# Squared-ReLU attention and a gated MLP on one core: 24 more score tiles of the first batch are written out and read back transposed, GpSimd copying their halves

## The chip, the cores and the metric

The kernel runs on one core of a Trainium2 chip. The time is the device time of one execution in microseconds (us). The engines are PE (TensorE), DVE (VectorE), ACT (ScalarE), POOL (GpSimd) and SP, whose instruction queue issues every transfer of this kernel.

## The reference

```python
scores = (1 / S) * z @ z.T            # per batch, S = 3008, z is S x 64
attn = maximum(scores, 0) ** 2
x = u * (attn @ v)                    # u and v are S x 256
xn = x / sqrt(mean(x * x) + 1e-6) * rms_g
y = (silu(xn @ w_gate) * (xn @ w_val)) @ w_out    # d_ff = 1536
```

There are four batches, and z, u and v are float32. The three weight matrices arrive as float64 and are used as two float32r parts each (a high and a low part), and so is every other operand of a product.

Scores are symmetric, so the tile of rows k and columns q is the transpose of the tile of rows q and columns k. The kernel makes use of that.

## The kernel before, in words

The tokens of a batch are cut into 6 chunks of 512 columns (the last has 448), and a chunk's keys into 24 tiles of 128 rows (the last has 64). A **step** is one key tile of one chunk; there are 4 x 6 x 24 = 576 steps, numbered i, and a program written out by hand goes through them in order. What an engine or SP's queue gets is in program order, and each works through its own queue in order.

In iteration i the program emits, in this order: the scores of step i + 3 (`emit_s`, L274 on: two matmuls at L284 and L285, the ReLU on ACT at L287 into a tile r, of which there are three); the preparation parts due at i (`stages`); the splitting of step i + 2 (`emit_l`, L296 on); the loads due at i (`loads`); a part of the MLP (`emit_g`, `emit_v`, `emit_y`), two iterations to one hidden tile of 128, from iteration 56 on; and the six matmuls of step i that multiply by v (`emit_av`, L342, L343, L347). In the first 80 steps most tiles are squared on ACT in `emit_l` (L302 writes H, L303 squares r in place); for the others DVE multiplies (L289) and ACT casts (L305). DVE subtracts the high part (L308, L313 for the last key tile).

**Kept tiles.** `keeps(b, c, kc)` names the groups of four key tiles (kc) that chunk c writes out for later: for these, behind the subtraction in `emit_l`, ACT copies the square r as two planes of 16-bit halves into a tile `halves` (L321; two buffers, which the result tiles y share), and SP's queue writes `halves` to device memory (L323, 256 KB). Chunk kc later needs the transpose of this block, in its four steps of key group c (`is_turned`, L259), and computes no score there: `load_turned` (L264 on) reads two steps at once with a transposing transfer into a tile T, six steps ahead, and L284 to L289 fall away. Before the change, `keeps` holds from step 72 on: 12 tiles of the first batch and 60 of each other batch (192 copies, 192 turned steps).

**Weights.** Each of the 18 pieces of weights is loaded by SP's queue (L114, 512 KB, into one of three buffers that T shares) in the loads of an iteration a - 3 and decoded and split in iterations a - 1 to a + 2. The first part is a square on ACT (`magnitude`, L122), then come seven instructions on DVE (L126 to L143) and a cast on ACT (L137). With a = 21, 25, 29, 33, 37, 41, 45, 49, 53, and then every second iteration to 71, the loads stand in iterations 18, 22, 26, 30, 34, 38, 42, 46, 50, 52, ..., 68. The moving operand z of the next chunk (`prep_mov`, L168) is loaded in iterations 18, 42 and 66, ahead of the weights of that iteration, and split on DVE (L173, L175) two iterations later. The u of a chunk (L357) is loaded at its 19th step.

A piece of the order in which `emit_l` and the loads are emitted, on which SP's queue depends:

```python
run(stages, i)
if i + LA <= nsteps and not ends:
    emit_l(i + LA - 1)
run(loads, i)
```

Of the kernel before, what the change touches and what calls it, by code (L numbers as in the profile page):

```python
# [12 lines left out]
U16 = mybir.dt.uint16  # L13
# [17 lines left out]
def kernel(  # L31
# [13 lines left out]
    nc = tc.nc  # L45
# [6 lines left out]
    NK = -(-S // P)  # L52
    NC = -(-S // CH)
# [4 lines left out]
    SKEW = 16  # L58
# [23 lines left out]
    def f32(ap):  # L82
        return ap.bitcast(F32)
# [170 lines left out]
    def keeps(b, c, kc):  # L254


        return (b * NC + c) * NK + 4 * kc >= NK + 3 * SKEW

    def is_turned(i):  # L259
        ci, kt = steps[i]  # L260
        b, c = chunks[ci][:2]
        return kt // 4 < c and keeps(b, kt // 4, c)
# [29 lines left out]
    def is_square(i):  # L292

        return i < 2 * NK + 2 * SKEW and (i % 6 != 5 if i < NK else i % 8 != 7)

    def emit_l(i):  # L296
        ci, kt = steps[i]
        b, c, t0, n = chunks[ci]
        a = att[i]
        hi = moving.tile([P, CH], F32R, tag="H", name="H", bufs=LA)  # L300
        if is_square(i):
            nc.scalar.activation(hi[:, :n], a[:, :n], AF.Square)  # L302
            nc.scalar.activation(a[:, :n], a[:, :n], AF.Square)  # L303
        else:
            nc.scalar.copy(hi[:, :n], a[:, :n])  # L305
        if kt < NK - 1:
            lo = moving.tile([P, CH], F32R, tag="L", name="L", bufs=LA)
            nc.vector.tensor_tensor(lo[:, :n], a[:, :n], f32(hi[:, :n]), op=ALU.subtract)  # L308
        else:

            lo = None
            h = slice(TAIL, P)
            nc.vector.tensor_tensor(hi[h, :n], a[h, :n], f32(hi[h, :n]), op=ALU.subtract)  # L313
        att[i] = (hi, lo)
        kc = kt // 4
        if kc > c and keeps(b, c, kc):
            if kt % 4 == 0:
                kept[b, kc, c] = dram.tile([2 * CH, CH], U16, tag=f"kept{kc}{c}", name=f"kept{kc}{c}")
            m = P if kt < NK - 1 else TAIL
            halves = work.tile([P, 2, CH], U16, tag="out", name="halves", bufs=2)  # L320
            nc.scalar.copy(halves[:m], a[:m].bitcast(U16).rearrange("p (q h) -> p h q", h=2))  # L321
            r0 = 2 * (kt % 4) * P
            nc.sync.dma_start(  # L323
                out=kept[b, kc, c][r0:r0 + 2 * m, :].rearrange("(p h) q -> p h q", h=2), in_=halves[:m]
            )
# [230 lines left out]
    def moe_at(fs):  # L556

        ci, f = divmod(fs, NF)
        return (ci, f) if 0 <= ci < len(chunks) else None
# [9 lines left out]
    with tc.manual_schedule():  # L569
# [12 lines left out]
        for i in range(LA):  # L582
            emit_s(i)
            if i:
                emit_l(i - 1)
            if early:
                run(stages, early.pop(0))
        for i in range(nsteps + 2 * (SKEW + NF + 1)):
# [9 lines left out]
# [3 lines that stand above are left out]
            m = moe_at(fs)  # L601
# [5 lines left out]
            m = moe_at(fs - 1)  # L607
# [8 lines left out]
            if ends:  # L616
                emit_gate(ci)
                if i + LA <= nsteps:
                    emit_l(i + LA - 1)
                for k, part in enumerate(norm_jobs(ci)):  # L620
                    stages[i + 1 + k].append(part)
# [33 lines left out]
```

## Time and profile before

| | us |
|---|---|
| median of 3 runs | 2138.23 (2137.46 to 2138.39) |
| the profiled execution | 2138.34 |
| its span, first to last instruction | 2136.6 |
| busy: PE, DVE, ACT, POOL | 2114.5, 1308.3, 1165.3, 0.2 |

The profiled execution lies within the three runs, and 1.7 us of it lie outside the span. Busy time is the share of the span in which an engine had an instruction running. Matmuls overlap each other in the profile: one is shown with 390 ns, but they start about 225 ns apart. An idle time is put down to the last thing that the instruction behind it waited for.

### The profile page before, as it was taken

The numbers are of one execution on the slowest core, as the hardware profiler recorded it, in microseconds if no ns is written. First come the engines' busy times: TensorE is split into PE (matmuls) and PEld (weight loads), VectorE is DVE, ScalarE is ACT, GpSimd is POOL, SyncE is SP. The second block draws the span as 40 slices with busy tenths as digits, with TensorE's granted clock in tenths as the row PEclk, the third lists the DMA queues.
The fourth block names the chain that finished last, engine by engine and source line by source line (L and its number), as shares of the span: only waits on it lengthen the run. The fifth ranks groups of instructions, "written<-read, shape, count | busy, mean of one in ns | idle before, by whom it ended". The sixth has DMA issues, their size and how long they took to land.

```text
span 2136.6 us, 25456 instructions
## 1 busy us (share of the span) xinstructions
PE 2114.5 (99%) x9408; PEld 1762.6 (82%) x9408; DVE 1308.3 (61%) x2361; ACT 1165.3 (55%) x1979; POOL 0.2 (0%) x4
## 2 busy tenths in 40 slices
PE   8899999999999999999999999999999999999999
PEld 7677888888888888888888888888888888888888
DVE  7988655775565555576655555557656565555543
ACT  8876555446574554545756545444666564544332
POOL 0000000000000000000000000000000000000000
PEclk9999999999999999999999999999999999999999
DMA  4211021322241415261313143244131332415100
GB/s 134 75 59 45 25 57 39 89 65 79 62 118 42 116 44 107 54 150 51 108 44 106 44 96 87 65 106 114 65 87 56 85 93 56 101 51 100 27 11 19
DMA packets 255660, 156.78 MB, mean 73 GB/s; under 512 B 198256, under 2 KB 213744, under 8 KB 255536
## 3 DMA queue, kind: packets, MB, share of 16 engines
q1 hardware_dynamic: 255536, 155.16, 26.8%
q8 instruction: 73, 1.20, 0.2%
q14 instruction: 51, 0.42, 0.1%
HBM read 46.60 MB, written 60.42 MB: 50 GB/s over the span
## 4 chain that ended last, share of the span: by engine, by line
PE 93%; DVE 4%; ACT 2%; issue 1%; DMA 0%; DVEq 0%
PE ps L460 12%; PE ps L461 12%; PE ps L463 12%; PE po L343 11%; PE po L342 11%; PE po L347 11%; PE py L496 6%; PE py L498 6%; PE py L497 6%; PE ps L285 4%; PE ps L284 4%; DVE L L308 1%; DVE wraw L128 0%; ACT H L302 0%; DVE wraw L141 0%
## 5 line engine op out<-in xcount | busy, mean ns | idle before, releaser
L482 ACT CAST hH<-s 128x512 fp32r<-128x512 f32 (+1 forms) x288 | 176.2, 612 | 526.0 <-DVE s L481 525.8
L342 PE MATMUL po<-H,vh 128*128 128x512 f32 (+1 forms) x1152 | 445.3, 387 | 0.0
L343 PE MATMUL po<-H,vl 128*128 128x512 f32 (+1 forms) x1152 | 445.2, 386 | 0.0
L289 DVE TENSOR_TENSOR r<-ps,r 128x512 f32<-128x512 f32 (+1 forms) x315 | 215.0, 683 | 309.2 <-ACT r L287 309.0
L287 ACT ACTIVATE r<-ps 128x512 f32<-128x512 f32 (+1 forms) x384 | 227.0, 591 | 278.6 <-PE ps L285 275.1
L347 PE MATMUL po<-L,vh 128*128 128x512 f32 (+1 forms) x1104 | 338.4, 388 | 5.6 <-DVE L L308 5.5
L483 DVE TENSOR_TENSOR hL<-s,hH 128x512 fp32r<-128x512 f32 (+1 forms) x288 | 196.2, 681 | 195.3 <-ACT hH L482 195.3
L481 DVE TENSOR_TENSOR s<-ps,s 128x512 f32<-128x512 f32 (+1 forms) x288 | 194.3, 675 | 191.4 <-PE ps L463 191.0
L308 DVE TENSOR_TENSOR L<-r,H 128x512 fp32r<-128x512 f32 (+1 forms) x360 | 243.8, 677 | 31.9 <-ACT r L303 20.4
L342 PEld LDWEIGHTS po<-H,vh 128*128 128x128 f32 x1152 | 216.8, 188 | 42.0 <-DVE H L313 0.4
L343 PEld LDWEIGHTS po<-H,vl 128*128 128x128 f32 x1152 | 216.9, 188 | 41.5
L347 PEld LDWEIGHTS po<-L,vh 128*128 128x128 f32 x1104 | 206.1, 188 | 51.2 <-DVE L L308 13.4
L496 PE MATMUL py<-hH,woh 128*128 128x512 f32 (+1 forms) x576 | 223.7, 388 | 4.4 <-ACT hH L482 4.3
L460 PE MATMUL ps<-xh,wvh 128*128 128x512 f32 (+1 forms) x576 | 224.5, 390 | 0.0
L498 PE MATMUL py<-hL,woh 128*128 128x512 f32 (+1 forms) x576 | 223.4, 388 | 0.0
L461 PE MATMUL ps<-xh,wvl 128*128 128x512 f32 (+1 forms) x576 | 222.4, 386 | 0.0
L470 ACT ACTIVATE s<-ps 128x512 f32<-128x512 f32 (+1 forms) x288 | 169.8, 590 | 96.3 <-PE ps L463 82.7
L497 PE MATMUL py<-hH,wol 128*128 128x512 f32 (+1 forms) x576 | 222.3, 386 | 0.0
L461 PE MATMUL ps<-xh,wgl 128*128 128x512 f32 (+1 forms) x576 | 222.2, 386 | 0.0
L460 PE MATMUL ps<-xh,wgh 128*128 128x512 f32 (+1 forms) x576 | 222.2, 386 | 0.0
L321 ACT COPY halves<-r 128x1024 uint16<-128x1024 uint16 x192 | 201.0, 1047 | 3.6 <-DMA out_T<-y 3.6
L305 ACT CAST H<-r 128x512 fp32r<-128x512 f32 (+1 forms) x315 | 191.3, 607 | 0.2 <-PE po L343 0.2
(81 smaller groups left out, 2655.5 us busy)
## 6 DMA issues: line engine op xcount, KB each, us to landing
kept<-halves SPq DMA_DIRECT2D x175, 256.0 KB, 2.0
raw<-in_v SPq DMA_DIRECT2D x44, 256.0 KB, 2.8
ux<-in_uT SPq DMA_DIRECT2D x40, 256.0 KB, 3.0
out_T<-y SPq DMA_DIRECT2D x40, 256.0 KB, 2.0
raw<-in_zT SPq DMA_DIRECT2D x39, 256.0 KB, 3.0
wraw<-in_w_gate SPq DMA_DIRECT2D x6, 512.0 KB, 5.4
wraw<-in_w_val SPq DMA_DIRECT2D x6, 512.0 KB, 3.5
wraw<-in_w_out SPq DMA_DIRECT2D x6, 512.0 KB, 3.2
```

Of the source, the lines that this page charges most:

```text
L287: nc.scalar.activation(a[:, :n], ps[:, :n], AF.Relu)
L289: nc.vector.tensor_tensor(a[:, :n], ps[:, :n], a[:, :n], op=ALU.mult)
L308: nc.vector.tensor_tensor(lo[:, :n], a[:, :n], f32(hi[:, :n]), op=ALU.subtract)
L342: nc.tensor.matmul(po[d][:, :n], wh[:, j, ds], hi[:, :n], start=(kt == 0), stop=False)
L343: nc.tensor.matmul(po[d][:, :n], wl[:, j, ds], hi[:, :n], start=False, stop=(lo is None))
L347: nc.tensor.matmul(po[d][:, :n], wh[:, j, ds], lo[:, :n], start=False, stop=False)
L460: nc.tensor.matmul(ps[:, :n], hi[:, d, fs], xsplit[ci, d][0][:, :n], start=(d == 0), stop=False)
L461: nc.tensor.matmul(ps[:, :n], lo[:, d, fs], xsplit[ci, d][0][:, :n], start=False, stop=False)
L463: nc.tensor.matmul(ps[:, :n], hi[:, d, fs], xsplit[ci, d][1][:, :n], start=False, stop=(d == ND - 1))
L496: nc.tensor.matmul(py[d][:, :n], woh[:, f, ds], hi[:, :n], start=(f == 0), stop=False)
L497: nc.tensor.matmul(py[d][:, :n], wol[:, f, ds], hi[:, :n], start=False, stop=False)
L498: nc.tensor.matmul(py[d][:, :n], woh[:, f, ds], lo[:, :n], start=False, stop=(f == NF - 1))
```

## The change

It makes `keeps` true for the groups kc = 4 and 5 of the first batch in every chunk, where it was true from step 72 on, and leaves the other batches as they are. New are the key tiles 16 to 23 of the chunks 0, 1 and 2 (steps 16 to 23, 40 to 47 and 64 to 71). The halves of the steps before 72 are copied by GpSimd in place of ACT; those are the 24 new ones and no others.

```diff
     def keeps(b, c, kc):
 
 
-        return (b * NC + c) * NK + 4 * kc >= NK + 3 * SKEW
+        return b > 0 or kc >= 4
 
     def is_turned(i):
         ci, kt = steps[i]
@@ -318,7 +318,9 @@
                 kept[b, kc, c] = dram.tile([2 * CH, CH], U16, tag=f"kept{kc}{c}", name=f"kept{kc}{c}")
             m = P if kt < NK - 1 else TAIL
             halves = work.tile([P, 2, CH], U16, tag="out", name="halves", bufs=2)
-            nc.scalar.copy(halves[:m], a[:m].bitcast(U16).rearrange("p (q h) -> p h q", h=2))
+
+            copy = nc.gpsimd.tensor_copy if i < 3 * NK else nc.scalar.copy
+            copy(halves[:m], a[:m].bitcast(U16).rearrange("p (q h) -> p h q", h=2))
             r0 = 2 * (kt % 4) * P
             nc.sync.dma_start(
                 out=kept[b, kc, c][r0:r0 + 2 * m, :].rearrange("(p h) q -> p h q", h=2), in_=halves[:m]
```

## Rows read from the trace of the kernel before

**Rows 1.** The page, busy time of each engine over the span.
```profile
PE 2114.5 (99%) x9408; PEld 1762.6 (82%) x9408; DVE 1308.3 (61%) x2361; ACT 1165.3 (55%) x1979; POOL 0.2 (0%) x4
```

**Rows 2.** Windows over steps 16-23, 40-47, 64-71: stretch, length, busy by engine, clock, DMA.
```profile
37.50:51.00 13.50, 12.82 (x56) 10.06 (x55) 11.46 (x20) 12.12 (x22) 0.00 (x0) 1.00 0.54 194
90.64:105.00 14.36, 11.20 (x43) 7.84 (x43) 13.20 (x23) 12.37 (x24) 0.00 (x0) 0.94 0.49 167
160.50:187.00 26.50, 26.16 (x109) 19.45 (x107) 22.01 (x39) 18.05 (x33) 0.00 (x0) 1.00 0.27 90
```

**Rows 3.** The chain that ended last, 92 to 95 us: start, length, piece.
```profile
92.92 0.57 ACT woh L122
93.49 0.53 ACT H L302
94.04 0.64 ACT r L303
94.70 0.69 DVE L L308
```

**Rows 4.** Timeline of DVE, L364 at a chunk's end: batches 0 and 1, chunks 3-5.
```profile
291.48 1.28 DVE L364 TENSOR_TENSOR ux<-po,ux 128x512 f32<-128x512 f32 x2
381.84 1.28 DVE L364 TENSOR_TENSOR ux<-po,ux 128x512 f32<-128x512 f32 x2
468.26 1.15 DVE L364 TENSOR_TENSOR ux<-po,ux 128x448 f32<-128x448 f32 x2
819.63 1.28 DVE L364 TENSOR_TENSOR ux<-po,ux 128x512 f32<-128x512 f32 x2
904.64 1.28 DVE L364 TENSOR_TENSOR ux<-po,ux 128x512 f32<-128x512 f32 x2
987.25 1.15 DVE L364 TENSOR_TENSOR ux<-po,ux 128x448 f32<-128x448 f32 x2
```

**Rows 5.** Timeline of PE, two score matmuls of 512 columns in chunk 4.
```profile
339.41 0.39 PE L284 MATMUL ps<-mh,zst 128*128 128x512 f32 x1
339.63 0.39 PE L285 MATMUL ps<-ml,zst 128*128 128x512 f32 x1
```

**Rows 6.** Groups of instructions, first 500 us: operation, shapes, count, busy, mean ns, idle before.
```profile
L308 DVE TENSOR_TENSOR L<-r,H 128x512 fp32r<-128x512 f32 (+1 forms) x136 | 92.0, 677 | 21.8 <-ACT r L303 20.4 <-ACT H L305 0.9 <-PE ps L285 0.3
L321 ACT COPY halves<-r 128x1024 uint16<-128x1024 uint16 (+1 forms) x19 | 19.9, 1046 | 0.0
```

**Rows 7.** Timeline of SP's queue (start, length, issue), and L114's time to landing, first 200 us.
```profile
41.48 0.90 SPq L114 DMA_DIRECT2D wraw<-in_w_gate  x2
...
90.02 0.94 SPq L357 DMA_DIRECT2D ux<-in_uT  x2
91.01 0.42 SPq L168 DMA_DIRECT2D raw<-in_zT  x1
91.49 2.42 SPq L114 DMA_DIRECT2D wraw<-in_w_gate  x2
...
DMA to landing us min/median/max: 3.1/3.4/7.6
```

**Rows 8.** Timeline of ACT around the first weight squares (L122) in the kept stretches.
```profile
44.04 0.63 ACT L303 ACTIVATE r<-r 128x512 f32<-128x512 f32 x1
...
47.47 0.67 ACT L122 ACTIVATE wgh<-wraw 128x512 fp32r<-128x512 f32 x1 [0.34 <-DMA wraw<-in_w_gate]
...
90.01 0.63 ACT L303 ACTIVATE r<-r 128x512 f32<-128x512 f32 x1
...
92.81 0.68 ACT L122 ACTIVATE woh<-wraw 128x512 fp32r<-128x512 f32 x1
...
98.46 0.63 ACT L303 ACTIVATE r<-r 128x512 f32<-128x512 f32 x1
...
101.14 0.66 ACT L122 ACTIVATE wgh<-wraw 128x512 fp32r<-128x512 f32 x1
...
168.18 0.63 ACT L303 ACTIVATE r<-r 128x512 f32<-128x512 f32 x1
...
174.65 0.66 ACT L122 ACTIVATE wvh<-wraw 128x512 fp32r<-128x512 f32 x1
```

**Rows 9.** Windows, 103 to 106 us, columns as in rows 2.
```profile
103.00:106.00 3.00, 2.71 (x7) 1.99 (x7) 2.90 (x6) 1.10 (x2) 0.00 (x0) 0.56 0.32 131
```

## The prediction

> **What bounds the kernel now.** The page comes first: PE is busy for 99% of the span and GpSimd does nothing [rows 1]. A score less is therefore worth its time on PE wherever PE really is the limit. But the copies that pay for it lie in the first 190 us, so I read that stretch apart. In the windows over the three stretches of new copies DVE is busy 11.46 of 13.50, 13.20 of 14.36 and 22.01 of 26.50 us, and ACT nearly as much in the first two [rows 2]. The chain of waits in the second goes from a weight square on ACT (L122) through the squares of a step to L308 on DVE, without PE [rows 3]. So here ACT and DVE set the pace, in turn, and a wait put on either is paid at the end. The chunks 4 and 5, where scores go, are bound by PE: its matmuls follow each other at 0.22 us [rows 5].
>
> **The gain: 24 turned steps in chunks 4 and 5.** `is_turned` asks the same function as `emit_l`, so the count is sure: 48 matmuls go, 24 of 512 columns and 24 of 448. The profile holds the very case: batch 1 already turns all these steps. From the end of chunk 3 to the end of chunk 4 it takes 904.64 - 819.63 = 85.01 us in batch 1 and 381.84 - 291.48 = 90.36 us in batch 0; chunk 5 takes 82.61 and 86.42 us [rows 4]. The difference is 5.35 + 3.81 = **9.2 us**. The other way, 24 x 0.22 + 24 x 0.22 x 448/512, gives 9.9 (10.2 with 0.227 us, since the rows are rounded) [rows 5]. I take 9.2. The 24 ReLUs, 24 multiplications and 12 transposing loads that change there lie beside PE as they do in batch 1; the loads come six steps ahead, and their blocks were written some 150 us before.
>
> **How long is a GpSimd copy?** No row shows one. The same copy on ACT takes 1.046 us; DVE does 512 elements in 0.677, so 1024 would take 1.35 [rows 6]. I take 1.4, the plain one-element-at-a-time pace, nearest to a copy of 1024 small elements; the ends are 1.05 and 2.7 (half that pace). The Trainium skill, "GPSIMD Engine Reference", "Performance versus the Vector engine", measures 512 elements of a one-input loop at 769 ns; doubled, that is an estimate of 1.54 us, which would add 0.14 to each lateness below. ACT saves nothing here, since these copies were not on it.
>
> **The wait that the change adds: weight loads behind a kept write.** SP's queue gets the kept write of step i + 2 ahead of the loads of iteration i, and the write waits for the copy. Before, SP ran far ahead: the first weights were issued at 41.48 us, and a weight pair at 91.49, which is when the u load in front of it let go [rows 7]; one late item holds all behind it. Now the load of iteration 18 stands behind the write of step 20, that of 38 behind step 40 and that of 42 behind step 44. Each lands after: end of r + copy 1.4 + issue 0.4 (0.4 more where the z load stands between) + 3.4 to land [rows 7]. Against the start of L122, which waits in ACT's queue ahead of the next steps' squares [rows 8]:
> - iteration 18: r ends 44.67, landing 44.67 + 1.4 + 0.8 + 3.4 = 50.3; L122 stood at 47.47: 2.8 us late.
> - iteration 38: 90.64 + 1.4 + 0.4 + 3.4 = 95.8 against 92.81: 3.0 late, and this L122 is in the chain [rows 3].
> - iteration 42: 99.09 + 1.4 + 0.8 + 3.4 = 104.7 against 101.14: 3.6 late.
>
> Together 9.4 us. The z load of 18 and 42 lands 0.4 us ahead of the weights and is wanted by DVE in the same iteration: inside the same stall. Behind the late square wait H and r of the step, L308, the weight's own seven DVE instructions and PE, which all lack it, so I count **9.4 us** in full. With the lower copy and the shortest landing (3.1) it is 3 x 0.65 less, 7.4; with a copy of 2.7 it is 13.3, and one landing of 7.6 would make it 17.5. The loads of 22 and 46 have two more iterations behind the last kept write: nothing. In chunk 2 steps last longer: r ends at 168.81, landing 174.0, L122 at 174.65 [rows 8]; four such loads are just in time, 0; at 2.7 us a copy they cost some 0.6 each. The u and v loads of chunk 0 come one or two copies later and are needed steps later: nothing.
>
> **GpSimd beside DVE.** Copy and L308 are released by the same end of r and read the same tile. Whether they slow each other no row shows. Lower end 0: the copies on ACT leave L308 at its 677 ns [rows 6]. Upper end: the two never overlap. Then 24 x 1.4 = 33.6 us of copies must fit into DVE's idle time, 2.04 + 1.16 + 4.49 = 7.7 [rows 2], and into the 9.4 us of stalls, and 16.5 us are left over; at 2.7 us a copy, 44. I take **5**, nearer to zero, as the only row of a copy says, but not zero, because the two start together each time.
>
> **Smaller terms.** PE's granted clock was 0.56 in the window behind a pause of PE near 102 us [rows 9]: seven matmuls there took about 0.43 in place of 0.225 us, 1.4 us. The first two new pauses may each do this, beside ACT and DVE: 0 to 2.8, taken **1.4**. The r tile must be free for the ReLU three steps on, some 1.85 us after its end; a copy of 1.4 fits (0), one of 2.7 would hold up 16 steps by 0.85, 14 us. The 24 writes of 256 KB share the rings with loads: DMA is busy 54% at most [rows 2]; inside the landing times.
>
> **Sum.** -9.2 + 9.4 + 5 + 1.4 = +6.6. The profiled execution took 2138.34 us, 1.7 beyond its span of 2136.6 and 0.1 above the median of the runs, so **2145.0 us**. A measurement of this kernel tells 0.2%, 4.3 us, from no change; this is just beyond.
>
> **The rivals.**
> *The two engines exclude each other.* For it: common start, DVE 85 to 92% busy. Against it: nothing in the profile shows any such exclusion. Its price is the upper end above: -9.2 + 9.4 + 16.5 + 1.4 = +18, **2156 us**; with copies of 2 us some 14 more. It decides once DVE loses over half a copy each time. The Trainium skill, "SBUF — State Buffer", "Who interferes with whom", says just this: a VectorE instruction with two SBUF inputs, or in a two-port mode, and a GpSimd instruction that reads SBUF exclude each other for the whole of whichever starts first. L308 and the weight arithmetic have two such inputs. No run here shows it yet. By that rule I would say 2156, and I give it a good chance. 0.27.
> *They cancel.* No effect on DVE and no lost clock: -9.2 + 9.4 = 0, **2138 us**. For it: L308's constant duration. 0.17.
> *Faster: the idle time takes up the stalls.* ACT has 1.38 and 1.99 us idle in the first two stretches [rows 2], waiting for others; if a late L122 only takes the place of these waits, and copy and landing are at their short ends, 7.4 - 3.4 = 4.0 us remain of the stalls and with the gain at 10.2 the result is -6.2, **2132 us**. It decides when the three stalls and all else cost under 4.9. Against it: L122 lies in the chain itself [rows 3]. 0.21.
> That the change does something else than it says is ruled out by the common function. 0.
>
> **How the numbers follow.** The forecast's own case, stalls and a mild hindrance of DVE, runs from +4.3 to +12 (2142.6 to 2150) and gets 0.35. Slower: 0.35 + 0.27 = 0.62; within 0.2%: 0.17; faster: 0.21. The range must take in the faster rival and most of the excluding one with copies of up to 2 us: **2132 to 2170**; below lies a full gain without stalls, above it copies of 2.7 us, about a tenth each.
>
> **What would show it.** Right: 24 GpSimd copies near 1.4 us; SP's weight loads of iterations 18, 38 and 42 issued right behind kept writes; ACT idle for about 3 us in front of three L122, released by the DMA; the ends of chunks 4 and 5 9 us closer together; L308 beside a copy a little longer than 677 ns or started later. The end of chunk 2 would come some 16 us later than before. Wrong: L122 never waiting for a load; L308 lengthened by a whole copy (then the first rival); chunks 4 and 5 unchanged.

## The result, and the profile after

The changed kernel takes 2151.84 us (median; 2151.09 to 2152.18), the kernel before 2137.85 on the same chip: a ratio of 1.0064, 95% interval 1.0052 to 1.0076, or some **14 us slower**. The profiled execution has a span of 2149.9 us, 13.3 more than before.

The page's busy times [rows 1]: 48 matmuls are gone, GpSimd works for 32.5 us, and DVE is busy for longer although 24 of its multiplications fell away.

```profile
PE 2106.6 (98%) x9360; PEld 1752.5 (82%) x9360; DVE 1314.0 (61%) x2337; ACT 1153.5 (54%) x1955; POOL 32.7 (2%) x28
```

The timeline of DVE, the line at the end of each chunk (L366 now), chunks 0 to 5 of batch 0 [rows 4]:

```profile
63.78 1.28 DVE L366 TENSOR_TENSOR ux<-po,ux 128x512 f32<-128x512 f32 x2
128.81 1.28 DVE L366 TENSOR_TENSOR ux<-po,ux 128x512 f32<-128x512 f32 x2
223.71 1.28 DVE L366 TENSOR_TENSOR ux<-po,ux 128x512 f32<-128x512 f32 x2
314.00 1.28 DVE L366 TENSOR_TENSOR ux<-po,ux 128x512 f32<-128x512 f32 x2
399.02 1.28 DVE L366 TENSOR_TENSOR ux<-po,ux 128x512 f32<-128x512 f32 x2
481.63 1.15 DVE L366 TENSOR_TENSOR ux<-po,ux 128x448 f32<-128x448 f32 x2
```

From one end to the next, in us (chunk 0 from the span's start). The kernel before has its ends at 56.31, 111.71, 199.91 and then as in [rows 4]. The runs told of below have their lines here too, by the names they have there:

| kernel | 0 | 1 | 2 | 3 | 4 | 5 |
|---|---|---|---|---|---|---|
| before | 56.31 | 55.40 | 88.20 | 91.57 | 90.36 | 86.42 |
| changed | 63.78 | 65.03 | 94.90 | 90.29 | 85.02 | 82.61 |
| Loads early | 61.96 | 60.13 | 94.90 | 90.30 | 85.02 | 82.61 |
| Copies alone | 60.74 | 60.77 | 94.88 | 91.62 | 90.36 | 86.41 |
| Chunk 2 on ACT | 63.32 | 65.11 | 89.40 | 90.31 | 85.02 | 82.60 |
| VectorE copies | 63.36 | 65.81 | 94.56 | 90.34 | 85.02 | 82.61 |
| Both mends (early, GpSimd and ACT) | 62.08 | 59.86 | 88.59 | 90.28 | 85.01 | 82.61 |
| Only chunk 2 (on ACT) | 56.23 | 55.39 | 88.41 | 89.77 | 88.55 | 84.77 |
| VectorE in chunks 0 and 1 (early, ACT in chunk 2) | 62.95 | 59.50 | 89.15 | 90.32 | 85.02 | 82.62 |
| Half copies | 57.84 | 57.15 | 91.52 | 91.61 | 90.36 | 86.42 |
| Memsets | 57.53 | 54.63 | 90.13 | 91.59 | 90.36 | 86.42 |
| ACT throughout (early) | 63.24 | 61.29 | 88.74 | 90.28 | 85.02 | 82.60 |
| All mended | 60.59 | 59.25 | 88.24 | 88.49 | 85.02 | 82.61 |

The change loses 7.47 + 9.63 + 6.70 = 23.8 us in chunks 0 to 2 and wins 1.28 + 5.34 + 3.81 = 10.4 in chunks 3 to 5. The two leave 13.4 us, against 13.3 between the spans.

Two things are new in chunks 0 to 2. First, ACT waits for weights. The timelines of ACT (L122, the first weight square; in brackets the idle time before it) and of SP's queue (L325 is the kept write, L168 the z load, L114 the weight load) show the three places [rows 7, 8]:

```profile
53.99 0.69 ACT L122 ACTIVATE wgh<-wraw 128x512 fp32r<-128x512 f32 x1 [4.60 <-DMA wraw<-in_w_gate]
...
103.57 0.66 ACT L122 ACTIVATE woh<-wraw 128x512 fp32r<-128x512 f32 x1 [2.45 <-DMA wraw<-in_w_out]
...
119.03 0.67 ACT L122 ACTIVATE wgh<-wraw 128x512 fp32r<-128x512 f32 x1 [5.37 <-DMA wraw<-in_w_gate]
```

```profile
48.16 0.34 SPq L325 DMA_DIRECT2D kept<-halves  x1
48.62 0.37 SPq L168 DMA_DIRECT2D raw<-in_zT  x1
49.03 0.45 SPq L114 DMA_DIRECT2D wraw<-in_w_gate  x1
...
99.29 0.34 SPq L325 DMA_DIRECT2D kept<-halves  x1
99.74 0.38 SPq L114 DMA_DIRECT2D wraw<-in_w_out  x1
...
113.06 0.34 SPq L325 DMA_DIRECT2D kept<-halves  x1
113.44 0.43 SPq L168 DMA_DIRECT2D raw<-in_zT  x1
114.32 0.33 SPq L114 DMA_DIRECT2D wraw<-in_w_gate  x1
```

A kept write stands in front, in the first and the third with the z load between, as the prediction had it. The first weights were issued at 41.48 us before, at 49.03 now.

Second, DVE and GpSimd stand in each other's way. The timelines of DVE and of GpSimd over two copies in chunk 2, where no load is late:

```profile
177.69 0.68 DVE L308 TENSOR_TENSOR L<-r,H 128x512 fp32r<-128x512 f32 x1
178.29 1.53 DVE L141 TENSOR_TENSOR wraw<-wraw,wgh 128x512 f32<-128x512 f32 x1
179.74 0.41 DVE L126 TENSOR_SCALAR wt<-wraw 128x512 uint32<-128x512 uint32 x1
180.07 1.52 DVE L143 TENSOR_TENSOR wgl<-wraw 128x512 fp32r<-128x512 f32 x1
181.52 0.68 DVE L128 SCALAR_TENSOR_TENSOR wraw<-wraw,wt 128x512 uint32<-128x512 uint32 x1
```

```profile
177.70 1.57 POOL L323 COPY halves<-r 128x1024 uint16<-128x1024 uint16 x1 [54.03 <-ACT r L303]
179.86 1.19 POOL L323 COPY halves<-r 128x1024 uint16<-128x1024 uint16 x1 [0.58 <-ACT r L303]
```

L141 and L143 take 1.53 and 1.52 us in place of 0.69. The first copy is shown from 177.70 on, beside L308, behind which L141 starts at 178.29; the copy ends at 179.27, and L141 ends 0.55 later, at 179.82. So the shown durations hold a wait: copy behind L308, L141 behind the copy. The copies' durations in the first 230 us agree (count, minimum, median and maximum in ns):

```profile
L323 POOL COPY halves<-r x24: 1042/1452/1572, 37.5 to 209.0; 128x1024 uint16<-128x1024 uint16 x21, 64x1024 uint16<-64x1024 uint16 x3
```

The least, 1.04 us, is a copy with nothing in its way. Each copy here costs DVE 1.53 - 0.69 = 0.84 us, and eight of them 6.7, which is the whole loss of chunk 2 (6.70).

### The profile page after: what moved, and what is told of

The parts are those of the page before. It is cut to its first block, busy times and chain, and to the rows that moved or that the text cites. A ratio compares the mean times of both kernels' runs of the same rounds, so it can differ in the third digit from the quotient of the medians.

```text
span 2149.9 us, 25445 instructions
## 1 busy us (share of the span) xinstructions
PE 2106.6 (98%) x9360; PEld 1752.5 (82%) x9360; DVE 1314.0 (61%) x2337; ACT 1153.5 (54%) x1955; POOL 32.7 (2%) x28
## 4 chain that ended last, share of the span: by engine, by line
PE 91%; DVE 4%; ACT 2%; issue 1%; DMA 1%; POOL 0%; SPq 0%; DVEq 0%; ACTq 0%; POOLq 0%
PE ps L462 12%; PE ps L463 12%; PE ps L465 12%; PE po L345 11%; PE po L344 11%; PE po L349 10%; PE py L498 6%; PE py L500 6%; PE py L499 6%; PE ps L284 3%; PE ps L285 3%; DVE L L308 1%; ACT H L302 1%; DVE wraw L128 1%; ACT r L287 1%
## 5 line engine op out<-in xcount | busy, mean ns | idle before, releaser
L289 DVE TENSOR_TENSOR r<-ps,r 128x512 f32<-128x512 f32 (+1 forms) x291 | 199.3, 685 | 285.6 <-ACT r L287 285.2
L287 ACT ACTIVATE r<-ps 128x512 f32<-128x512 f32 x360 | 213.3, 593 | 254.9 <-PE ps L285 248.7
L308 DVE TENSOR_TENSOR L<-r,H 128x512 fp32r<-128x512 f32 x336 | 232.3, 692 | 34.4 <-ACT r L303 22.3
L498 PE MATMUL py<-hH,woh 128*128 128x512 f32 (+1 forms) x576 | 223.6, 388 | 12.1 <-ACT hH L484 12.1
L305 ACT CAST H<-r 128x512 fp32r<-128x512 f32 (+1 forms) x291 | 177.3, 609 | 0.2 <-PE po L345 0.2
```

The costliest lines, as they stand in the source:

```text
L287: nc.scalar.activation(a[:, :n], ps[:, :n], AF.Relu)
L498: nc.tensor.matmul(py[d][:, :n], woh[:, f, ds], hi[:, :n], start=(f == 0), stop=False)
```

## The experiments

**Loads early.** It takes the late weights away and leaves the copies.

```diff
-            plan(prep_w(*w), at - 1, 2)
+            plan(prep_w(*w), at - 1, 8 if at < NK + 2 * SKEW - 3 else 2)
```

> The changed kernel with the first eight weight loads issued six iterations earlier (8 instead of 2 iterations ahead of their first use), so that none of them stands behind the kept write of the step that it needs. Theory: two costs add up, the late loads (ACT waited 4.6, 2.5 and 5.4 us for them, 12.1 us more than before) and GpSimd's copies holding up VectorE (the rest of the 23.8 us lost in chunks 0 to 2, 11.7 us). Then those waits go and the time falls by 8 to 12 us, to 2140 to 2144 us, still slower than before (2137.9). Rival, exclusion alone: the stalls only hide the copies, which then hold up VectorE for as long; the time falls by under 4 us, 2148 us or more. Rival, loads alone: back to the full gain, about 2128 us.

2144.72 us, ratio to the kernel before 1.0032 (1.0020 to 1.0044): 7.1 less than the changed kernel. No L122 waits for a transfer any more. The 12.1 us of waits were worth 7.1 by the times and 6.7 by the chunks (chunk 0: 1.8, chunk 1: 4.9, chunk 2: nothing), just below the theory's 8. That part of the waits had covered time that DVE loses to the copies anyway is the likely reason; it was not measured by itself. What lies behind is still slower than before, so loads alone (2128) is out, and so is exclusion alone.

**Copies alone.** The other half by itself, added to the kernel before, with no gain and no new transfers.

```diff
+        if kc > c and kc >= 4 and not keeps(b, c, kc):
+            m = P if kt < NK - 1 else TAIL
+            halves = work.tile([P, 2, CH], U16, tag="out", name="halves", bufs=2)
+            nc.gpsimd.tensor_copy(halves[:m], a[:m].bitcast(U16).rearrange("p (q h) -> p h q", h=2))
```

> The kernel before plus the 24 GpSimd copies and nothing else: no kept writes of them and no turned steps, so no gain and no late load. Theory: VectorE is held up once per copy by about 0.84 us (1.53 in place of 0.69 us for one instruction beside each), 24 x 0.84 = 20 us less what VectorE's idle time takes up: plus 12 to 18 us, 2150 to 2156 us. Rival (the copies hinder VectorE little, the loads are all): plus 5 us or less, below 2143 us.

2154.95 us, ratio 1.0080 (1.0063 to 1.0097): **16.5 us** for copies that nobody reads. By chunk 4.4, 5.4 and 6.7. This and the 7.1 of the loads make up the 23.8 us lost, but for 0.2 (but for 0.6 by the chunks). DVE's groups in the first 210 us, two-input instructions beside copies (mean ns at the end; 687, 690 and 689 in the kernel before):

```profile
L308 DVE TENSOR_TENSOR L<-r,H 128x512 fp32r<-128x512 f32 x69 | 52.1, 760 | 14.8 <-ACT r L303 14.1 <-PE ps L285 0.5
L143 DVE TENSOR_TENSOR wol<-wraw 128x512 fp32r<-128x512 f32 x4 | 3.5, 868 | 0.1
L143 DVE TENSOR_TENSOR wgl<-wraw 128x512 fp32r<-128x512 f32 x6 | 5.8, 969 | 0.1
```

What part has TensorE's clock in it? The windows over chunk 2, first of "loads early", then of this run, bear on it (columns as in rows 2): the granted clock is 1.00 in one and 0.96 in the other, DVE is busy equally long, and the chunk takes the same time, so the lower clock shows no cost there. Busy DVE explains the length: 76.24 us in chunk 2 of the kernel before, 83.00 here.

```profile
122.09:216.99 94.90, 81.44 (x335) 60.62 (x333) 83.00 (x142) 59.83 (x110) 10.98 (x8) 1.00 0.26 79
121.51:216.39 94.88, 84.11 (x335) 62.85 (x333) 83.00 (x142) 59.83 (x110) 10.89 (x8) 0.96 0.18 59
```

**Half copies.** The same with one of the two planes, half the elements: does the cost go by the copy's length or by the meeting?

```diff
-            nc.gpsimd.tensor_copy(halves[:m], a[:m].bitcast(U16).rearrange("p (q h) -> p h q", h=2))
+            nc.gpsimd.tensor_copy(halves[:m, 0, :], a[:m].bitcast(U16).rearrange("p (q h) -> p h q", h=2)[:, 0, :])
```

> The kernel before plus 24 GpSimd copies of one of the two planes, half the elements of a full copy (no kept writes, no turned steps, as in the run of copies alone, which lost 16.5 us). Theory (a VectorE instruction beside a copy waits for the copy's length): about half of a full copy's 1.04 us alone, so some 0.3 to 0.5 us per copy are lost on VectorE in place of 0.84, plus 6 to 10 us, 2144 to 2148 us. Rival (each meeting of the two costs a fixed time, whatever the length): plus 13 us or more, 2151 us or above.

2145.16 us, ratio 1.0035 (1.0021 to 1.0049), 6.8 us for 24 half copies. The least duration of a copy fell from 1.04 to 0.62 us, the lengthened L141 from 1.53 to 1.10. In chunk 2 3.3 us are lost in place of 6.7. The cost goes by the length.

**Memsets.** Does GpSimd have to read for it? A memset of the same tile in place of the copy, started by a tiny VectorE copy so that it begins just behind L308.

```diff
-            nc.gpsimd.tensor_copy(halves[:m], a[:m].bitcast(U16).rearrange("p (q h) -> p h q", h=2))
+            nc.vector.tensor_copy(halves[:m, 0, :2], a[:m, :1].bitcast(U16))
+            nc.gpsimd.memset(halves[:m], 0)
```

> The run of copies alone with each GpSimd copy replaced by a GpSimd memset of the same 128x1024 tile, which reads nothing; a VectorE copy of two elements of r into the tile goes before it, so that it starts at the same place (24 times some 0.17 us on VectorE). It tells whether the exclusion needs GpSimd to read. Theory (it is the read that VectorE's second input waits for): the instructions of VectorE with two tensor inputs (L141, L143, L128, L136) keep their 0.69 us beside a memset, and the time is 2 to 6 us above the kernel before, 2140 to 2145 us. Rival (any GpSimd instruction that uses the memory excludes VectorE's): they are lengthened as beside a copy, and 12 us or more are lost, 2150 us or above. The Trainium skill, "SBUF — State Buffer", "Who interferes with whom", says that an instruction with two inputs contends with a GpSimd instruction that reads, not with one that only writes, while a two-port one (the casts and tensor-scalar instructions of 0.42 us) contends with both.

2141.56 us, ratio 1.0016 (1.0006 to 1.0025): 3.4 us, with the 24 tiny copies (0.17 each) in it. By chunk 1.2, -0.8 and 1.9. DVE's groups as above:

```profile
L308 DVE TENSOR_TENSOR L<-r,H 128x512 fp32r<-128x512 f32 x73 | 50.1, 687 | 16.5 <-ACT r L303 16.4
L126 DVE TENSOR_SCALAR wt<-wraw 128x512 uint32<-128x512 uint32 x18 | 9.0, 501 | 0.0
L143 DVE TENSOR_TENSOR wol<-wraw 128x512 fp32r<-128x512 f32 x6 | 4.1, 690 | 0.1
```

And one place in the timelines, first GpSimd's memset, then DVE:

```profile
170.60 0.95 POOL L320 MEMSET halves<- 128x1024 uint16 x1 [3.90 <-DVE halves L319]
170.44 0.69 DVE L141 TENSOR_TENSOR wraw<-wraw,wgh 128x512 f32<-128x512 f32 x1
171.04 0.79 DVE L126 TENSOR_SCALAR wt<-wraw 128x512 uint32<-128x512 uint32 x1
```

L141, with two inputs, runs beside the memset in its usual 0.69 us; L126, an instruction of 0.42 us with one input, takes 0.79. So it is GpSimd's read that the two-input instructions wait for, and the quick one-input instructions wait for a write as well.

**Chunk 2 on ACT.** Is there an engine with room?

```diff
-            copy = nc.gpsimd.tensor_copy if i < 3 * NK else nc.scalar.copy
+            copy = nc.gpsimd.tensor_copy if i < 2 * NK else nc.scalar.copy
```

> The changed kernel with the eight copies of chunk 2 on ACT again, GpSimd keeping those of chunks 0 and 1. In chunk 2 ACT waits about 4.4 us in every two steps for VectorE, so two copies of 1.05 us fit. Theory (in chunk 2, which has no late load, the copies on GpSimd cost 6.7 us through VectorE alone): minus 5 to 7 us, 2145 to 2147 us, the end of chunk 2 coming as much earlier. Rival (those 6.7 us come from the writes and loads on SP's queue, whichever engine copies): unchanged, 2150 to 2153 us.

2145.89 us, ratio 1.0039 (1.0026 to 1.0052), 6.0 below the changed kernel: chunk 2 now loses 1.2 us in place of 6.7, with the same writes on SP's queue. The rival is out.

**VectorE copies.** All 24 on DVE (`nc.vector.tensor_copy` in that line).

> The changed kernel with the 24 copies on VectorE itself in place of GpSimd. Theory (a copy on GpSimd costs VectorE some 0.84 us, as if it were VectorE's own): with a copy of 0.55 us on VectorE 2144 to 2149 us, with one of 1.1 us 2153 to 2160 us, so between minus 8 and plus 8 us of the changed kernel. Rival (beside GpSimd VectorE loses little): VectorE's own copies come on top, 24 x 1.1 = 26 us, 2165 us or more.

2151.56 us, ratio 1.0064 (1.0049 to 1.0079): the same as with GpSimd, so handing the copies to GpSimd had won nothing in all over doing them on DVE. A copy takes 0.69 us on DVE, and the next instruction starts 0.60 us after it. The loads come later still here, and ACT's waits for them sum to 18.1 us (12.4 with GpSimd).

**Both mends.** Loads early and chunk 2 on ACT, GpSimd in chunks 0 and 1.

> The changed kernel with both mends of the runs before: the first eight weight loads six iterations earlier, and the copies of chunk 2 on ACT (GpSimd keeps those of chunks 0 and 1). Theory: the two add up, since they lie in different chunks: 2151.8 - 7.1 - 6.0 = 2138.7 us, no change against the kernel before (2137 to 2140). Rival (the two share a cause, so that the second mend adds little): 2143 us or more.

2138.89 us, ratio 1.0005 (0.9996 to 1.0015): they add up, and 13 of the 14 us are back; but the gain is all spent.

**VectorE in chunks 0 and 1.** "Both mends" with DVE in GpSimd's place there.

> All 24 tiles kept, nothing on GpSimd: the copies of chunks 0 and 1 on VectorE (0.69 us each, a new instruction every 0.60 us there, in place of some 0.84 us lost beside a copy on GpSimd), those of chunk 2 on ACT, the first eight weight loads six iterations earlier. Theory: 16 x 0.24 = 4 us less than the run with the same loads, GpSimd in chunks 0 and 1 and ACT in chunk 2 (2138.7), so 2134 to 2137 us. Rival (the copy on VectorE stands in the queue between a step's subtraction and the next, and holds r and the later work as much as GpSimd did): 2138 us or more.

2138.77 us, ratio 1.0003 (0.9994 to 1.0012): a miss, the rival's number. Against "both mends" chunk 0 lost 0.9, chunk 1 won 0.4, and chunk 2, with the same copies in both, lost 0.6. PE waited 9.5 us in chunks 0 and 1 for the split of z (L173 on DVE), against 2.5 before. The z load still comes behind a kept write, but DVE itself waited only 1.9 us for it, and in "copies alone", which has no new kept write, PE waited 5.6 us for the split and DVE for no z load: DVE comes to the split late, and the load is the smaller part.

**ACT throughout.** Loads early, all copies on ACT.

> All 24 copies on ACT, with the first eight weight loads six iterations earlier. Theory: ACT is busy about 90% in chunks 0 and 1 and takes turns with VectorE in the chain, so 16 copies of 1.05 us cost there nearly their length, 14 us less ACT's idle 3.4 us, in place of the 9.4 us that the same chunks lose with GpSimd: 2138.9 + 1 to + 5, 2140 to 2144 us. Rival (ACT has room, and only VectorE is short): 2136 us or less.

2141.01 us, ratio 1.0014 (1.0005 to 1.0024), as expected: chunks 0 and 1 lose 6.9 and 5.9 us with ACT against 5.8 and 4.5 with GpSimd in "both mends". With none of the three engines do they come near their old length. How much of that is the copy and how much its write was measured for GpSimd only (4.4 and 5.4 us by the copies alone).

**Only chunk 2.** The kernel before with the one stretch in which an engine has room.

```diff
-        return (b * NC + c) * NK + 4 * kc >= NK + 3 * SKEW
+        return b > 0 or c >= 2
```

> The kernel before with only chunk 2 of the first batch kept in addition (its key tiles 12 to 23, 12 tiles), the copies on ACT, nothing on GpSimd, chunks 0 and 1 as before. Theory: a copy costs what its engine is short of in that stretch, and ACT has some 4 us to spare in every two steps of chunk 2, so 12 copies cost 1 to 2 us and 12 turned steps in chunks 3 to 5 give 5 us: minus 3 to 4 us, 2134 to 2136 us, faster than both kernels. Rival (kept writes in front of weight loads cost as much as in chunks 0 and 1): no faster than before.

**2132.99 us, ratio 0.9976 (0.9967 to 0.9986)**: faster than both kernels, a little more than expected. Chunk 2 loses 0.2 us for 12 copies, and chunks 3 to 5 win 1.8 + 1.8 + 1.65 us. The windows from 130 to 200 us show where the copies went (columns as in rows 2), this kernel first, then the kernel before: ACT is busy for 12.4 us more and PE for as long as before.

```profile
130.00:200.00 70.00, 65.37 (x264) 49.18 (x262) 59.67 (x112) 56.00 (x92) 0.00 (x0) 0.98 0.39 121
```

```profile
130.00:200.00 70.00, 65.49 (x265) 49.29 (x263) 59.83 (x113) 43.60 (x80) 0.00 (x0) 0.98 0.20 64
```

**All mended.** Chunk 2 as there, chunks 0 and 1 on DVE, loads early, and each kept write behind the loads of its iteration, which is the piece shown:

```diff
             run(loads, i)
+            flush()
```

(`flush` issues the kept writes that `emit_l` has put on a list.)

> All of chunk 2 kept (12 tiles, copies on ACT) and the 16 tiles of chunks 0 and 1 (copies on VectorE), the first eight weight loads six iterations earlier, and each kept write issued behind the loads of its iteration in place of ahead of them, so that the z loads of iterations 18 and 42 go one step earlier too. With the same copies in chunks 0 and 1, PE still waited 9.5 us for the split of z there (2.5 us before the change). Theory: that wait is most of what these chunks still lose, 3 to 5 us of it go, and 4 more tiles in chunk 2 give 1.8 us: 2138.8 - 5 to - 7, 2132 to 2134 us, about as fast as with chunk 2 alone (2133.0). Rival (VectorE's own copies are what chunks 0 and 1 lose): 2136 to 2138 us, slower than with chunk 2 alone.

2134.13 us, ratio 0.9980 (0.9971 to 0.9989). Chunks 0 and 1 still lose 4.3 and 3.9 us, 8.1 together, for 16 tiles that give 7. PE's wait for the split of z fell from 9.5 to 6.7 us only, and DVE's own wait for the z load from 1.9 to 1.4, so the z load was the smaller part of it; of the two theories neither is cleanly met. What these chunks still lose stays open. The kernel beats the other two, but not chunk 2 alone (its interval and that of "only chunk 2" overlap).

## Why the prediction was right, and where its size was off

The direction, the range (2132 to 2170) and the places were right; the time given, 2145.0, is 6.8 us below the measured one. The range held the times of all three rivals too (2132, 2138, 2156), so that the measured one lies in it says little for the forecast's own case, which ended at 2150. Chunk 2 ended 23.8 us later than before, where 16 were forecast. Step by step:

- **The gain, 9.2: measured 10.4.** Chunks 4 and 5 took 85.02 and 82.61 us, as in batch 1. What was left out is 1.28 us in chunk 3: scores are emitted three steps ahead, so chunk 4's first three lie before the end of chunk 3 (six matmuls at 0.22 us are 1.3). The count of matmuls, 10.2, had it.
- **The copy, 1.4 us: mean 1.36.** Right by chance. Alone it takes 1.04, like ACT's copy; the rest is waiting.
- **The late loads, 9.4: waits of 12.1, worth 7.1.** The three places are those named. In each a landing took longer than the 3.4 us assumed, 4.9 us for the first (issued at 49.03, L122 at 53.99), 3.8 and 4.7 us for the others. Over a third of the waits cost nothing in the end. That chunk 2's loads come just in time (0) was right.
- **GpSimd beside DVE, 5 (between 0 and 16.5): measured 16.5 alone.** This is the step that was mis-sized. "I take **5**, nearer to zero, as the only row of a copy says" rested on copies on ACT, which say nothing about GpSimd. The truth is the first rival, "the two engines exclude each other", whose 2156 lies nearer to the 2151.8 measured. The sign that it named for this rival was only in part the right one: L308 itself grew little (mean 760 ns against 687 in "copies alone"), since it has mostly begun when the copy's turn comes, and the instruction behind it waits. That the loss alone equals the upper end is luck: of 24 x 1.04 = 25.0 us of copies 8.5 cost nothing, where the upper end had 17.1 of 33.6 cost nothing, 9.4 of them in stalls that "copies alone" does not have. ("DVE 85 to 92% busy" holds for the first two stretches; in the third it is 83% [rows 2].)
- **The clock, taken 1.4.** Of two new falls one is there: the granted clock was 0.72 from 52 to 58 us, behind 6 us in which PE was busy for 3.46; before, it was 1.00 there, behind 5.32 us of 6. It is 0.72 there in "loads early" and in "copies alone" too, so the late load is not what brings it. The fall behind the third late load (0.71 from 118 to 125 us) is one that the kernel before has at the same steps [rows 9]. What the new fall cost was not measured by itself; in chunk 2 a lower clock showed no cost (0.96 against 1.00, 94.88 and 94.90 us).
- **The sum:** -10.4 + 7.1 + 16.5 = +13.2, against 13.3 in the spans.

The rule that the prediction weighed, from the Trainium skill, "SBUF — State Buffer", "Who interferes with whom", fits the meetings shown here: two-input instructions wait for a copy that reads (1.53 in place of 0.69 us) and not for a memset (0.69), the one-input instructions of 0.42 us wait for both (L126 takes 1.26 us at 106.05 beside a copy, 0.79 beside a memset), and the wait grows with the length of the copy. The 769 ns of "GPSIMD Engine Reference" in the Trainium skill are a loop's of that page and not a copy's, and the estimate of 1.54 us worked out from them was too long: alone the copy took 1.04.

## What to carry to other kernels

A transfer that waits for a computed tile, put into an in-order queue, delays every load behind it: look at what follows it and by when that is needed, and issue such loads ahead of it. An engine that stands idle is no free engine if its instructions hold up those of the one that is short; price the move by what it takes from the busy engine (here 0.84 us beside a copy in chunk 2 and 0.69 in the mean, against 0.60 for doing the copy there), and measure it: in the whole kernel the two came out alike (2151.84 and 2151.56; 2138.89 and 2138.77 with both mends). And where a reuse costs one copy per tile, compare per tile and per stretch: a turned tile gave 0.43 us (10.4 / 24), a copy on GpSimd cost 0.69 (16.5 / 24), and one on ACT, where ACT had room, 0.02 (0.2 / 12; in "chunk 2 on ACT" up to 0.15, 1.2 / 8). So 12 tiles in the one roomy stretch were a better change than 24 in all three.

## What the runs showed of the hardware that was not expected

- GpSimd copies 1024 16-bit elements per partition in 1.04 us, as fast as ACT (1.05), and sets them in 0.95; DVE copies them in 0.69.
- The time that an instruction waits for the other engine is shown as its own duration, on both engines: the copies' median of 1.45 us and L141's 1.53 hold some 0.4 and 0.84 us of waiting. Idle time before an instruction does not show it.
- The exclusion is selective: an instruction with two inputs ran beside a memset undisturbed, a quicker one with one input did not. Which of the two waits goes by which is first: behind a memset that had begun, L126 took 0.79 us in place of 0.42; where L126 was first (at 96.69), it kept its 0.42 and the memset behind it took 1.16 in place of 0.95.
